# A pre-LayerNorm linear-attention and gated-GELU block on one core: centred first tiles with a ScalarE accumulator, a second ring for the weight tail, K weights first, joined late product groups

## The chip, the cores and the metric

The kernel runs on 1 core of one Trainium2 chip. The metric is device time in microseconds (us), as the median of several executions; "span" is the time from the first to the last instruction in a profiled execution, and is about 1.8 us shorter than the time of the same execution. A profile also gives the clock that the throttle granted TensorE; executions at clock 0.99 to 1.00 are called fast here and the one at clock 0.95 slow.

In the profile PE is TensorE's matmul stream, PEld its weight loads, DVE VectorE, ACT ScalarE, POOL GpSimd, and SPq the queue from which SyncE issues DMAs.

## The reference

Sequence 2048, width 448, 16 heads of 28, hidden width 1792, all in bfloat16.

```python
phi = lambda t: jnp.where(t > 0, t + 1, jnp.exp(t)) + 1e-6
q, k, v = split_heads(layernorm(x) @ wqkv)
pq, pk = phi(q), phi(k)
kv  = einsum("bhsd,bhse->bhde", pk, v)
den = einsum("bhqd,bhd->bhq", pq, pk.sum(s)) + 1e-6
h   = x + (einsum("bhqd,bhde->bhqe", pq, kv) / den) @ wo
y   = layernorm(h)
out = h + (gelu(y @ w_gate) * (y @ w_up)) @ w_down
```

## The kernel before

The sequence is cut into 16 tiles of 128 rows. The kernel makes a list of tasks, finds what depends on what from the buffers that they read and write, and places the tasks on each engine in a fixed order (five long lists of task numbers, one per engine). Each engine works through its list in order; a task that waits holds up all tasks behind it.

The head: statistics of each tile on VectorE, the reciprocal deviation on ScalarE (logarithm, then exponential), normalisation, and a transposition. Tiles 0 to 3 are transposed by TensorE, the others by a transposing DMA.

```python
def ln_tile(t):                                              # before
    ln_stats(t, ...)                                         # DVE: bn_stats, bn_aggr
    ln_rstd_act(t, ...)                                      # ACT: Ln, then Exp(-0.5 * .)
    if t < N_PE_TR:                                          # tiles 0..3
        op("dve", tensor_scalar(xnn, x_sb, mean, rstd, subtract, mult), "normD_t")
        # two transposes each on PE -> PSUM, evacuated by ACT ("evxA_t") and by DVE ("evxD_t")
    else:
        # GpSimd normalises ("normP_t"), a DMA transposes:
        G.add("sp", dma_start_transpose(xnT[:, t], xnn[:, i]), name="xT_t", after=[two])
# [cut]
def k_tile(t):
    # PE: K projection of tile t, 4 matmuls of 448 columns, "k_t"
    act_exp(activation(e1[:, i], psK, AF.Exp), "ek_t")
    op("dve", tensor_scalar(e1, e1, 1.0 + EPS, 0.0, min, max), "ck_t")
    op("dve", scalar_tensor_tensor(pk, psK, EPS, e1, max, add), "pk_t")
    # PE: x^T pk accumulated over the tiles, 4 matmuls, "pt4_t" (the last tiles: "pt3_t")
# [cut]  q_tile: projection "q_t", then ACT: Exp "eq_t" and Relu "rq_t"
```

After the last accumulation the sums are evacuated, the key-value product "kv" is made, masked to the heads, and multiplied with the output weights ("w2"). At the same time the denominators of the first tiles are started:

```python
op("act", ... "z1"); op("dve", ... "z0"); op("dve", ... "evpD_3")
# evpA_0, evpA_1 on ACT and evpD_2 on DVE bring the accumulated sums to SBUF; kv reads them all
# a2_pair: per pair of tiles
op("dve", tensor_scalar(eq, eq, 1.0, EPS, min, add), "cq_t")
op("dve", tensor_tensor(pq, pq, eq, add),            "aq_t")
op("dve" if t == 0 else "pool", tensor_tensor(t1, pq, zbc, mult), "t1_t")
op("dve", tensor_reduce(den, t1), "dr_t")
op("act", activation(den, den, AF.Identity, bias=eps), "deA_t")
```

The rest is a stream of attention outputs ("out"), gate/up pairs of 64-row matmuls ("gu", each pair on both halves of the array) and down projections ("down"). Between the last two, GpSimd normalises and VectorE copies a wrapped part of the row ("wrap_t").

## Time and profile before

| | value |
|---|---|
| time, median of 3 executions | 194.29 us (194.02 to 194.54) |
| profiled execution (slow) | 199.48 us, span 197.8 us, clock 0.95 |
| TensorE busy | 98% of the span |
| first projection starts (slow profile) | 6.31 us |
| key-value product starts (slow profile) | 38.76 us |

Of the page of the kernel before: the head line, TensorE's busy time, the granted clock by slices, the chain that ended last, and the costliest group of matmuls.

```profile
span 197.8 us, 4145 instructions
...
PE 193.7 (98%) x1572; PEld 106.9 (54%) x1572; DVE 132.0 (67%) x355; ACT 78.1 (39%) x226; POOL 50.7 (26%) x92
...
PEclk9999999999999999999999999999999999999999
...
PE 90%; DMA 4%; DVE 4%; POOL 1%; issue 0%; DVEq 0%; POOLq 0%
...
L605 PE MATMUL ps<-hnT,wgu_sb 64*128 64x512 bf16 (+1 forms) x490 | 89.9, 342 | 0.0
```

TensorE is the limit, and nearly all of the chain is TensorE. A change that leaves the products as they are can only take away waits. The clock row shows a 9 in every slice; the 0.95 comes from the run's list of cores. It can be seen in the matmuls too: one of 448 columns follows the next after 197 ns here and after 189 ns in the fast executions.

The timeline of the kernel before in the head (columns: start, duration, engine, line, operation, tiles, shapes; in brackets the idle time before and what ended it).

```profile
3.37 0.63 DVE L348 BATCH_NORM_STATS2 st<-x_sb 128x6 f32<-128x448 bf16 x1 [3.37 <-DMA x_sb<-in_A_x_dram]
...
4.24 0.29 ACT L355 ACTIVATE ln<-mv,eps_t 128x1 f32<-128x1 f32 x1 [1.75 <-DVE mv L349]
...
4.85 0.37 DVE L370 TENSOR_SCALAR xnn<-x_sb,mv,rs 128x448 bf16<-128x448 bf16 x1
...
5.37 0.38 PE L378 MATMUL ps<-ident,xnn 128*128 128x128 bf16 x4
...
6.31 0.74 PE L404 MATMUL ps<-wqk_sb,xnT 128*128 128x448 bf16 x3
```

From the landing of tile 0 at 3.37 us to the first projection at 6.31 us the work goes through VectorE, ScalarE, VectorE, TensorE, an evacuation and TensorE again. This is the stretch that the change attacks.

### The profile page before, as it was taken

What the parts mean: (1) busy time and instruction counts of PE and PEld (TensorE: products, weight loads), DVE (VectorE), ACT (ScalarE), POOL (GpSimd) and SP (SyncE); (2) the same over time, 40 slices, a digit from 0 to 9 for tenths busy, and PEclk for the clock granted to TensorE, in tenths of its full rate; (3) what the DMA queues carried; (4) which work ended last, traced back from release to release, by engine and by line L of the source; (5) the groups of instructions that cost most, each with busy time, mean ns of one, the idle gap of its engine ahead of it and who ended that gap; (6) DMA issues with size and microseconds to landing.
All of it is one profiled execution on the core that took longest, in us unless ns stands there. A gap on an engine that the chain in (4) does not pass through costs nothing.

```text
span 197.8 us, 4145 instructions
## 1 busy us (share of the span) xinstructions
PE 193.7 (98%) x1572; PEld 106.9 (54%) x1572; DVE 132.0 (67%) x355; ACT 78.1 (39%) x226; POOL 50.7 (26%) x92
## 2 busy tenths in 40 slices
PE   7999999999999999999999999999999999999995
PEld 7554555555767776654454445444444454444454
DVE  3899988999999989988786537244445422444412
ACT  3797645599943324141330420023444200334200
POOL 7067710640451955235222024000000000000000
PEclk9999999999999999999999999999999999999999
DMA  6966449994587046420217272600200010100011
GB/s 194 375 174 88 94 96 209 221 215 63 102 291 124 16 50 117 102 53 23 56 26 153 57 56 52 133 21 30 46 0 3 0 46 4 46 0 3 0 46 46
DMA packets 35331, 16.97 MB, mean 86 GB/s; under 512 B 27696, under 2 KB 34032, under 8 KB 35312
## 3 DMA queue, kind: packets, MB, share of 16 engines
q1 hardware_dynamic: 35168, 16.60, 38.4%
q8 instruction: 12, 0.20, 0.4%
q10 hardware_dynamic: 144, 0.11, 0.2%
q14 instruction: 7, 0.06, 0.1%
HBM read 8.26 MB, written 1.84 MB: 51 GB/s over the span
## 4 chain that ended last, share of the span: by engine, by line
PE 90%; DMA 4%; DVE 4%; POOL 1%; issue 0%; DVEq 0%; POOLq 0%
PE ps L603 42%; PE ps L575 22%; PE ps L404 9%; PE ps L523 7%; PE ps L423 5%; PE ps L605 3%; DMA x_sb<-in_A_x_dram 2%; DVE st L348 2%; DMA xnT<-xnn 2%; DVE pk L417 1%; PE ps L471 0%; PE ps L462 0%; POOL wqk_sb L302 0%; PE ps L550 0%; DVE xnn L370 0%; DVE mv L349 0%
## 5 line engine op out<-in xcount | busy, mean ns | idle before, releaser
L605 PE MATMUL ps<-hnT,wgu_sb 64*128 64x512 bf16 (+1 forms) x490 | 89.9, 342 | 0.0
L603 PE MATMUL ps<-hnT,wgu_sb 64*128 64x512 bf16 (+1 forms) x490 | 89.6, 342 | 0.0
L623 ACT ACTIVATE gl<-ps 128x256 bf16<-128x256 f32 x112 | 37.1, 381 | 88.5 <-PE ps L605 86.4
L603 PEld LDWEIGHTS ps<-hnT,wgu_sb 64*128 64x128 bf16 x490 | 46.3, 96 | 35.1 <-issue 3.1
L625 DVE TENSOR_TENSOR hh<-ps,gl 128x256 bf16<-128x256 f32 x112 | 42.5, 416 | 34.0 <-ACT gl L623 33.7
L605 PEld LDWEIGHTS ps<-hnT,wgu_sb 64*128 64x128 bf16 x490 | 45.2, 96 | 3.7 <-DVE hh L625 0.5
L575 PE MATMUL ps<-wd_sb,hh 128*128 128x448 bf16 (+1 forms) x238 | 45.2, 351 | 0.0
L575 PEld LDWEIGHTS ps<-wd_sb,hh 128*128 128x128 bf16 x238 | 23.3, 99 | 21.1 <-issue 1.3
L404 PE MATMUL ps<-wqk_sb,xnT 128*128 128x448 bf16 x128 | 28.2, 362 | 0.1
L488 POOL TENSOR_TENSOR t<-pq,zbc 128x448 f32<-128x448 bf16 x15 | 16.6, 1115 | 33.3 <-DVE pq L484 20.5
L579 DVE TENSOR_TENSOR x_sb<-ps,x_sb 128x448 bf16<-128x448 f32 (+1 forms) x17 | 10.0, 592 | 19.6 <-PE ps L575 19.6
L348 DVE BATCH_NORM_STATS2 st<-x_sb 128x6 f32<-128x448 bf16 x32 | 19.1, 612 | 3.5 <-DMA x_sb<-in_A_x_dram 3.4
L404 PEld LDWEIGHTS ps<-wqk_sb,xnT 128*128 128x128 bf16 x128 | 12.3, 99 | 12.1 <-DMA xnT<-xnn 0.5
L423 PE MATMUL ps<-pk,xnn 128*128 128x448 bf16 x64 | 14.4, 363 | 0.0
L523 PE MATMUL ps<-w,pqnT 112*128 112x448 bf16 x64 | 14.1, 362 | 0.0
L558 POOL TENSOR_SCALAR hn<-x_sb,nm,rs 128x448 bf16<-128x448 bf16 x14 | 10.9, 779 | 8.1 <-DMA hnT<-hn 7.4
L529 DVE TENSOR_TENSOR x_sb<-ps,x_sb 128x448 bf16<-128x448 f32 x16 | 9.5, 617 | 3.8 <-PE ps L523 3.8
L415 ACT ACTIVATE e<-ps 128x448 bf16<-128x448 f32 x16 | 8.7, 541 | 5.4 <-PE ps L404 3.6
L417 DVE SCALAR_TENSOR_TENSOR pk<-ps,e 128x448 bf16<-128x448 f32 x16 | 9.9, 616 | 0.2
L388 POOL TENSOR_SCALAR xnn<-x_sb,nm,rs 128x448 bf16<-128x448 bf16 x12 | 9.0, 749 | 3.5 <-ACT rs L357 3.5
L423 PEld LDWEIGHTS ps<-pk,xnn 128*128 128x128 bf16 x64 | 6.5, 101 | 6.2
L495 DVE TENSOR_TENSOR pqn<-pq,rd 128x448 bf16<-128x448 bf16 x16 | 9.6, 622 | 0.0
(65 smaller groups left out, 125.0 us busy)
## 6 DMA issues: line engine op xcount, KB each, us to landing
out_dram<-x_sb SPq DMA_DIRECT2D x15, 112.0 KB, 1.7
wd_sb<-in_B_w_down_dram SPq DMA_DIRECT2D x1, 1568.0 KB, 7.7
x_sb<-in_A_x_dram SPq DMA_DIRECT2D x3, 448.0 KB, 5.4
wgu_sb<-in_B_w_gate_dram SPq DMA_DIRECT2D x1, 896.0 KB, 11.9
wgu_sb<-in_B_w_up_dram SPq DMA_DIRECT2D x1, 896.0 KB, 16.5
wqk_sb<-in_A_wqkv_dram SPq DMA_DIRECT2D x1, 672.0 KB, 4.8
wgu_sb<-in_B_w_gate_dram SPq DMA_DIRECT2D x1, 672.0 KB, 6.0
wgu_sb<-in_B_w_up_dram SPq DMA_DIRECT2D x1, 672.0 KB, 8.4
```

Source lines behind the costliest of these rows:

```text
L348: op("dve", lambda e: e.bn_stats(st[:, t, :], src_ap), [b_src], [b_st[t]], "bnst%s_%d" % (tag, t))
L404: ins = e.matmul(ps[:, bk, 0:D], xnT[:, t, k, :], wqk_sb[:, k, c0:c0 + D], start=(k == 0), stop=(k == 3))
L417: op("dve", lambda e: e.scalar_tensor_tensor(pk[:, ip, :], psK, EPS, e1[:, i, :], ALU.max, ALU.add), [b_ps[bk], b_e1[i]], [b_pk[ip]], "pk_ ...
L423: ins = e.matmul(ps[:, BK_PT[c], 0:D], xnn[:, t % XN_R, c * 128:(c + 1) * 128], pk[:, ip, :], start=(t == 0), stop=(t == T - 1))
L488: op(eng, lambda e, t=t, n=n: e.tensor_tensor(t1[:, n, :], pq[:, t, :], zbc[:, :], ALU.mult), [b_pq[t]] + b_z, [b_t1[n]], "t1%s_%d" % (eng ...
L523: ins = e.matmul(ps[:, BK_OUT[n], 0:D], pqnT[0:GW, i2, n, g, :], w2[:, g, :], start=(g == 0), stop=(g == NG - 1))
L558: op("pool", lambda e, t=t, sh=sh: e.tensor_scalar(hn[:, sh, 0:D], x_sb[:, t, :], nm2[:, t:t + 1], rs2[:, t:t + 1], ALU.add, ALU.mult), [b ...
L575: ins = e.matmul(psO, hh[:, j, (t % HR) * 128:(t % HR + 1) * 128], wd_sb[:, j, c0:c1], start=(j == 0), stop=(j == NJ - 1))
L603: e.matmul(psG[:, jj * N:(jj + 1) * N], wgu_sb[A_, k, j * 128:(j + 1) * 128], hnT[A_, ka_, c0:c0 + N], start=(k == 0), stop=(k == NK - 1))
L605: ins = e.matmul(psU[:, jj * N:(jj + 1) * N], wgu_sb[B_, k, j * 128:(j + 1) * 128], hnT[B_, kb_, c0:c0 + N], start=(k == 0), stop=(k == NK ...
L623: G.add("act", lambda e, gi=gi, cs_=cs_, psG=psG: e.activation(gl[:, gi, cs_], psG[:, cs_], AF.Gelu_apprx_tanh), r=[b_ps[BK_G[i]]], w=[b_g ...
L625: op("dve", lambda e, dst=dst, srcU=srcU, srcL=srcL: e.tensor_tensor(dst, srcU, srcL, ALU.mult), [b_ps[BK_U[i]], b_glh], [b_ar[j_][t % HR] ...
```

## The change

Its intent: let TensorE start earlier and pause less.

1. Tiles 0 and 1 are only centred before the transposition; the reciprocal deviation becomes the per-partition scale of the later Exp and Relu. It drops out of the chain to the first projection. The K features of these two tiles then take a second ScalarE pass (rk_t) and an addition (pka_t). GpSimd normalises the two tiles besides (normP_0, normP_1), for the accumulation x^T pk.
2. Tile 1's statistics come from ScalarE's accumulator instead of VectorE.
3. The K half of the weights is loaded first, the weight tail goes by ScalarE's ring, and K0 and K1 are projected before Q0. The output weights are loaded after the transposing DMAs. The loads of x are cut smaller, and the padding of the weights moves from GpSimd to VectorE.
4. The orders of all engines are new. Late attention outputs stand next to down projections, so there are seven changes from full-height matmuls into the gate/up pairs and seven back, where there were nine and nine.

```diff
+    CEN = (0, 1)
+    ACT_ST = (1,)
-    WARM = 40
+    WARM, WARM2, NW2 = 30, 3, 3
-    SEQ = "Q0 K0 K1 Q1 K2 Q2 ..."
+    SEQ = "K0 K1 Q0 K2 Q1 Q2 ..."
@@ loads
-        dma_w3("sp", wqk_sb, 0, 2 * D, b_wqk, "dwqk")
-        dma_w1("sp", wqk_sb, 0, 2 * D, b_wqk, "dwqk_t")
-        dma_x("sp", 2, 4)
+        dma_wqk(1)
+        dma_w1("act", wqk_sb, 0, 2 * D, [None, b_wqt], "dwqk_t")
+        dma_x("sp", 2, 3)
+        dma_wqk(0)
+        dma_x("sp", 3, 4)
@@ ln_tile
+            if t in ACT_ST:
+                act_exp(... activation(e1[:, 2, :], x_sb[:, t, :], AF.Identity, scale=1.0 / D, accum_out=mv1[:, t, 0:1]) ... "asum")
+                act_exp(... activation(e1[:, 3, :], x_sb[:, t, :], AF.Square, scale=D ** -0.5, accum_out=mv1[:, t, 1:2]) ... "asq")
@@
+                if t in CEN:
+                    op("dve", ... tensor_scalar(xc[:, t % 2, 0:D], x_sb[:, t, :], mv1[:, t, 0:1], None, ALU.subtract) ... "cen")
@@ k_tile
+            sc = rs1[:, t:t + 1] if t in CEN else 1.0
+            if t in CEN:
+                act_exp(... activation(pk[:, ip, :], psK, AF.Relu, scale=sc) ... "rk")
+                op("dve", ... tensor_scalar(e1, e1, 1.0, EPS, ALU.min, ALU.add) ... "ck")
+                op("dve", ... tensor_tensor(pk, pk, e1, ALU.add) ... "pka")
[cut: q_tile the same way; ORDERS, five lists, are new throughout]
```

Three places of the new orders, given with the tasks' names in place of their numbers:

```diff
  VectorE, before:  cq_5 aq_4 aq_5 evpD_3 z0 t1_0 dr_0 rd_0 evpD_2 ...
  VectorE, after:   aq_4 evpD_3 cq_5 z0 aq_5 t1_0 dr_0 evpD_2 rd_0 ...
  TensorE, before:  k_8 pt4_5 pt4_6 k_9 k_10 pt4_7 ...
  TensorE, after:   k_8 pt4_4 k_7 pt4_5 k_9 k_10 pt4_6 ...
  ScalarE, after:   ek_0 rk_0 ek_1 ln1_3 rk_1 evxA_2 ...
```

## The prediction

> **What bounds the kernel now.** TensorE. The page has it busy 193.7 of 197.8 us; the chain of waits is 90% TensorE and stays on it from 18.3 to 195.4 us. In the list of its instructions matmuls start at stream pace (197 ns for 448 columns, 224 ns for a 512-column pair, at the granted clock 0.949). The profile is of a slow execution (199.48 us; timed runs 194.29), so I compare stages, not totals. The change leaves every product as it is: only the head and the bubbles can pay.
>
> **Where TensorE loses time** (start-to-start spacing less stream time):
> - Head: the first projection starts at 6.31 us. x tile 0 lands at 3.37; then statistics 0.63+0.18, logarithm and exponential 0.29+0.20, normalise 0.37, transposes, evacuation 0.38. Tile 1's normalise ends at 6.0. The QK weights land at 6.0, their tail at 6.3.
> - 0.28 us at 9.6 (normalised tile 3), 0.22 at 17.9 (transposing DMA of tile 7), 0.26 between 40 and 42.5.
> - Changes between full-height matmuls (attention output, down projection) and the 64-row gate/up pairs: nine into and nine out of the pairs, 92-105 ns each, 1.7 us together. The Trainium skill, "TensorEngine Tiling (Array Packing)", Key Properties, says that changing the tiling mode drains TensorE; these gaps agree.
>
> **What the change does.**
> 1. Tiles 0 and 1 are only centred; the reciprocal deviation becomes the scale of the later exp/relu. That takes 0.5 us of ScalarE and its hand-overs out of the head. Tile 1's sums go to ScalarE, idle then; VectorE saves 0.78 us. Half the weights (K) come first, so weights no longer bind. My sum: centring ends about 4.6 (tile 0) and 5.0 (tile 1); the warm-up matmuls (36 before the first transpose, 107 ns each from about 1.2) end about 5.05; transposes, evacuation 0.38: first projection at about 5.75, a gain of 0.55.
> 2. Given back in part: ScalarE gets two more 448-wide passes (0.43 us spacing each), VectorE still works without pause from 7 us; tile 3's normalised input comes about 10.4, a bubble near 0.35. At the first accumulation of K-features (11.78 before) I expect 11.3-11.5: gain 0.3-0.5.
> 3. The transposing DMAs start about when they did or slightly earlier, with the output projection's weights moved behind them; the 0.22 us bubble should go.
> 4. Joined groups: the two orders give seven changes into and seven out of the pairs. Four fewer at 95 ns: 0.38 us.
> 5. The end (last down projection, addition, store) is the same: 195.04 to 197.8.
>
> Sum: 0.4+0.2+0.4 = about 1.0 us, all on the critical path. **Predicted 193.3 us, range 192.2 to 194.5.** Chances: faster by over 2% 0.02, within 2% 0.96, slower by over 2% 0.02.
>
> **What would show it.** (1) First projection 5.6-5.9 us, K first. (2) First K-feature accumulation 11.3-11.5. (3) No gap over 100 ns for a transposing DMA near 18 us. (4) Seven gaps of about 95 ns into the pairs. (5) After the last pair eight down projections without a pause.
>
> **What would make it wrong.** TensorE's clock gate: the warm-up leaves half pace (107 to 56 ns per matmul) at 5.15 us. The Trainium skill, "TensorE: Matmul & The Clock Gate", Part 1, calls the window free-running (3.4 us), so an earlier start may run at half pace and save nothing. ScalarE's queue in the head may bind: projection banks come free later because two passes read each. A joined group may wait for an input that isn't ready, where before gate/up pairs filled the time. And a different granted clock in the timed runs moves the total as much as the change: 0.5% of clock is 0.9 us.

## More of the kernel before

In the run of the kernel before that was repeated later, the profile fell in a fast execution. Its timeline around the key-value product (L462) is the one to compare with:

```profile
35.15 0.39 DVE L450 COPY zbc<-zbc 64x448 f32<-64x448 f32 x1
35.57 0.62 DVE L488 TENSOR_TENSOR t<-pq,zbc 128x448 f32<-128x448 bf16 x1
35.62 2.48 POOL L488 TENSOR_TENSOR t<-pq,zbc 128x448 f32<-128x448 bf16 x2 [9.38 <-DVE zbc L450]
36.23 0.62 DVE L491 TENSOR_REDUCE den<-t 128x16 f32<-128x448 f32 x1
...
37.23 0.98 ACT L454 ACTIVATE pt_sb<-ps 128x448 bf16<-128x448 f32 x2
...
38.54 0.99 PE L462 MATMUL ps<-pt_sb,wv_sb 128*112 128x112 bf16 x16
```

VectorE's product for tile 0 (t1_0, the first L488) takes 0.62 us and starts just before GpSimd's for tile 1; the evacuations (L454) follow and the key-value product starts with no idle time in brackets.

## The result, and the profile after

The kernel after takes 195.12 us (median of 6, 194.93 to 195.19), the kernel before in the same rounds 194.27 us (194.02 to 194.76). The ratio is 1.0039 with a 95% interval of 1.0025 to 1.0053: within 2%, and slower by 0.4% where a gain of 0.5% was forecast; 195.12 lies outside the range. All ratios here are the mean time of one kernel's fast runs over that of the other's of the same rounds, so they are not quite the ratios of the quoted medians.

The profile after fell in a fast execution (195.09 us, clock 1.00). Of its page:

```profile
span 193.3 us, 4166 instructions
...
PE 187.3 (97%) x1571; PEld 112.7 (58%) x1571; DVE 132.5 (69%) x355; ACT 79.3 (41%) x232; POOL 51.9 (27%) x96
...
PE 89%; DVE 5%; ACT 2%; DMA 2%; issue 0%; SPq 0%; DVEq 0%; ACTq 0%
...
L648 PE MATMUL ps<-hnT,wgu_sb 64*128 64x512 bf16 (+1 forms) x490 | 86.5, 334 | 0.4 <-DVE hh L668 0.4
```

The span cannot be compared with the slow profile's 197.8 us. What can be read is the chain: ScalarE, absent before, is on it now with 2%. The last column of the last line has changed as well: gate/up matmuls idled 0.4 us for a product of VectorE, where the page before had 0.0.

The head of the kernel after:

```profile
3.32 0.63 DVE L365 BATCH_NORM_STATS2 st<-x_sb 128x6 f32<-128x448 bf16 x1 [1.71 <-DMA x_sb<-in_A_x_dram]
...
4.20 0.60 DVE L399 TENSOR_SCALAR xc<-x_sb,mv 128x448 bf16<-128x448 bf16 x2
...
5.05 0.39 PE L410 MATMUL ps<-ident,xc 128*128 128x128 bf16 x4
...
5.75 0.63 DVE L365 BATCH_NORM_STATS2 st<-x_sb 128x6 f32<-128x448 bf16 x1 [0.95 <-DMA x_sb<-in_A_x_dram]
...
5.89 0.54 PE L437 MATMUL ps<-wqk_sb,xnT 128*128 128x448 bf16 x2
...
6.30 0.27 DVE L417 COPY xnT<-ps 128x256 bf16<-128x256 bf16 x1
...
6.63 0.36 PE L437 MATMUL ps<-wqk_sb,xnT 128*128 128x448 bf16 x1 [0.20 <-DVE xnT L417]
```

The first projection starts at 5.89 us, as forecast. (Idle time in brackets counts from a modelled end of the matmul before; the waits that I quote are start-to-start spacing beyond the stream time of 189 ns for 448 columns, and come out larger by about 0.16 us.) After two of its four matmuls it stops: VectorE's half of the transposed tile (L417) stands behind the statistics of tile 2, whose rows had not landed before 5.7 us. From start to start the second matmul took 547 ns instead of 189: 0.36 us lost.

The next stop, at tile 2's projection, in the same timeline:

```profile
7.22 0.63 ACT L450 ACTIVATE e<-ps,rs 128x448 bf16<-128x448 f32 x1
...
7.75 0.63 ACT L452 ACTIVATE pk<-ps,rs 128x448 bf16<-128x448 f32 x1
...
8.27 0.64 ACT L450 ACTIVATE e<-ps,rs 128x448 bf16<-128x448 f32 x1
...
8.97 0.64 ACT L452 ACTIVATE pk<-ps,rs 128x448 bf16<-128x448 f32 x1
...
9.49 0.40 ACT L415 ACTIVATE xnT<-ps 128x256 bf16<-128x256 bf16 x1
...
9.94 0.93 PE L437 MATMUL ps<-wqk_sb,xnT 128*128 128x448 bf16 x4 [0.27 <-ACT xnT L415]
```

ScalarE goes through four scaled passes before it evacuates tile 2's transposes (L415); TensorE waits for that, 0.43 us from start to start beyond the stream time. And at the key-value product (L505):

```profile
35.15 0.39 DVE L493 COPY zbc<-zbc 64x448 f32<-64x448 f32 x1
35.57 0.39 DVE L527 TENSOR_TENSOR pq<-pq,eq 128x448 bf16<-128x448 bf16 x1
35.63 1.24 POOL L531 TENSOR_TENSOR t<-pq,zbc 128x448 f32<-128x448 bf16 x1 [9.82 <-DVE zbc L493]
35.88 1.46 DVE L531 TENSOR_TENSOR t<-pq,zbc 128x448 f32<-128x448 bf16 x1
...
37.38 0.62 DVE L534 TENSOR_REDUCE den<-t 128x16 f32<-128x448 f32 x1
...
38.03 0.31 ACT L536 ACTIVATE den<-den,eps_d 128x16 f32<-128x16 f32 x1 [2.60 <-DVE den L534]
...
38.25 0.96 ACT L497 ACTIVATE pt_sb<-ps 128x448 bf16<-128x448 f32 x2
...
39.30 1.00 PE L505 MATMUL ps<-pt_sb,wv_sb 128*112 128x112 bf16 x16 [0.67 <-DVE den L534]
```

Compare with the same place before. The addition aq_5 (L527) now stands between the copy z0 and t1_0. GpSimd's product for tile 1 is released by the copy as well and waits its turn beside aq_5, so it is next when aq_5 ends; VectorE's t1_0, recorded from 35.88 us, ends only 0.48 us after GpSimd's product and takes 1.46 us where it took 0.62. In the kernel before t1_0 came directly behind the copy, and it was GpSimd's product that took longer (1.48 us there; 1.04 us for most of the later ones). This holds in all 20 profiles: t1_0 took 1.46 us in the nine in which aq_5 stands between the copy and t1_0, and 0.62 to 0.63 us in the eleven in which it does not. Everything behind t1_0 moves: the reduction, ScalarE's addition of the epsilon (L536), which stands ahead of the two evacuations (L497), and the key-value product. TensorE waits 0.84 us. (The bracket of L505 names L534; of what the product reads, ScalarE's second evacuation, L497, ended last, at 39.21 us.)

The wait at tile 10, with the DMA queue's line for four transposing DMAs, tile 10's first:

```profile
19.74 5.33 SPq L423 DMA_TRANSPOSE xnT<-xnn  x4
...
23.34 0.92 PE L437 MATMUL ps<-wqk_sb,xnT 128*128 128x448 bf16 x4 [0.67 <-ACT e L450]
```

The bracket names a ScalarE pass, but the DMA of tile 10, issued at 19.74 us, landed at 23.21 us, 0.13 us before the projection started.

The sum of TensorE's waits up to the key-value product in this profile, each as start-to-start spacing beyond the stream time: 0.36 (first projection), 0.43 (tile 2), 0.18 (tile 5, for a ScalarE pass), 0.83 (tile 10, for its transposing DMA) and 0.84, together 2.64 us. In the fast profile of the kernel before they are 0.22, 0.08 and 0.93 (a transposing DMA again), 1.23 us. So 0.70 us of earlier start (5.89 instead of 6.59 in these two executions) are set against 1.41 us of new waits, and the key-value product starts 0.76 us later: 39.30 instead of 38.54. From there to the last matmul the kernel after takes 151.32 us and the kernel before 151.81.

### The profile page after: what moved, and what is told of

Its sections match the earlier page's. It is cut to its first block, busy times and chain, and to the rows that moved or that the text cites. A ratio compares the mean times of both kernels' runs of the same rounds, so it can differ in the third digit from the quotient of the medians.

```text
span 193.3 us, 4166 instructions
## 1 busy us (share of the span) xinstructions
PE 187.3 (97%) x1571; PEld 112.7 (58%) x1571; DVE 132.5 (69%) x355; ACT 79.3 (41%) x232; POOL 51.9 (27%) x96
## 4 chain that ended last, share of the span: by engine, by line
PE 89%; DVE 5%; ACT 2%; DMA 2%; issue 0%; SPq 0%; DVEq 0%; ACTq 0%
PE ps L646 30%; PE ps L618 22%; PE ps L648 13%; PE ps L437 10%; PE ps L566 7%; PE ps L463 5%; DMA x_sb<-in_A_x_dram 2%; ACT e L450 1%; DVE hh L668 1%; DVE t L531 1%; DVE hn L603 1%; DVE den L534 1%; ACT pk L452 1%; PE ps L505 1%; PE ps L514 0%; PE ps L593 0%
## 5 line engine op out<-in xcount | busy, mean ns | idle before, releaser
L648 PE MATMUL ps<-hnT,wgu_sb 64*128 64x512 bf16 (+1 forms) x490 | 86.5, 334 | 0.4 <-DVE hh L668 0.4
L646 PE MATMUL ps<-hnT,wgu_sb 64*128 64x512 bf16 (+1 forms) x490 | 86.4, 333 | 0.0
L646 PEld LDWEIGHTS ps<-hnT,wgu_sb 64*128 64x128 bf16 x490 | 45.3, 94 | 19.0 <-issue 2.6
L648 PEld LDWEIGHTS ps<-hnT,wgu_sb 64*128 64x128 bf16 x490 | 42.6, 94 | 9.9 <-DVE hh L668 5.7
L618 PE MATMUL ps<-wd_sb,hh 128*128 128x448 bf16 (+1 forms) x238 | 43.4, 342 | 0.0
L531 POOL TENSOR_TENSOR t<-pq,zbc 128x448 f32<-128x448 bf16 x15 | 16.0, 1079 | 34.8 <-DVE pq L527 19.8
L463 PE MATMUL ps<-pk,xnn 128*128 128x448 bf16 x64 | 13.7, 353 | 0.0
L566 PE MATMUL ps<-w,pqnT 112*128 112x448 bf16 x64 | 13.6, 353 | 0.0
L369 POOL TENSOR_SCALAR nm<-mv 128x1 f32<-128x1 f32 (+1 forms) x21 | 5.3, 257 | 29.1 <-DVE mv L366 28.7
L420 POOL TENSOR_SCALAR xnn<-x_sb,nm,rs 128x448 bf16<-128x448 bf16 x14 | 10.1, 724 | 5.6 <-ACT rs L374 4.2
L450 ACT ACTIVATE e<-ps 128x448 bf16<-128x448 f32 x14 | 7.6, 547 | 6.7 <-PE ps L437 5.2
```

What stands on the lines that cost most here:

```text
L420: op("pool", lambda e: e.tensor_scalar(xnn[:, i, 0:D], x_sb[:, t, :], nm1[:, t:t + 1], rs1[:, t:t + 1], ALU.add, ALU.mult), [b_x[t], b_nm1 ...
L463: ins = e.matmul(ps[:, BK_PT[c], 0:D], xnn[:, t % XN_R, c * 128:(c + 1) * 128], pk[:, ip, :], start=(t == 0), stop=(t == T - 1))
L531: op(eng, lambda e, t=t, n=n: e.tensor_tensor(t1[:, n, :], pq[:, t, :], zbc[:, :], ALU.mult), [b_pq[t]] + b_z, [b_t1[n]], "t1%s_%d" % (eng ...
L566: ins = e.matmul(ps[:, BK_OUT[n], 0:D], pqnT[0:GW, i2, n, g, :], w2[:, g, :], start=(g == 0), stop=(g == NG - 1))
L618: ins = e.matmul(psO, hh[:, j, (t % HR) * 128:(t % HR + 1) * 128], wd_sb[:, j, c0:c1], start=(j == 0), stop=(j == NJ - 1))
L646: e.matmul(psG[:, jj * N:(jj + 1) * N], wgu_sb[A_, k, j * 128:(j + 1) * 128], hnT[A_, ka_, c0:c0 + N], start=(k == 0), stop=(k == NK - 1))
```

## The experiments

There were eighteen runs, and every result was correct. "Order" diffs name tasks in place of their numbers. In each job the kernel before ran in the same rounds; its medians in the five jobs were 194.25, 194.06, 194.25, 194.22 and 194.59 us.

Theory H said that the loss is made in the head, up to the key-value product, and that the late reordering pays what was forecast for it. The rival, theory L, said that the joined late groups cost more than the saved mode changes. They are told apart by making each half alone.

### before_again and after_again

No edit; both kernels again, for a fast profile of the kernel before and for the spread.

> The kernel before, unchanged, to have its profile in the fast state (the first one was taken at a granted clock of 0.949, the kernel after at 1.0). Ratio 1.000 +- 0.002 on any theory. Theory A (my prediction read the bubbles off a slowed TensorE): at the full clock TensorE reaches every hand-over about 5% earlier and waits where the slow profile showed none; I expect a wait of 0.4 to 0.9 us before the key-value product (near 37 us) here too, a gap in the projections near 22 us, and more than 3 us lost in all, against 1.2 us outside the mode changes in the slow profile. Theory B (the change made new waits): none of those gaps is here, the key-value product starts without a wait as in the slow profile.

> The kernel after, unchanged, on the same chip as the three others, as a corner of a two-by-two comparison. All theories: ratio 1.003 to 1.005, as in the first measurement.

Measured: before_again 194.32 us, ratio 1.0004 (0.9984 to 1.0024). after_again 195.22 us, ratio 1.0056 (1.0040 to 1.0073), with the key-value wait and the 1.46 us of t1_0 as in the first profile. The loss repeats. Theory A of the first text falls in its main points: the kernel before has no wait at the key-value product at clock 1.00 either, and of its waits up to there, 1.23 us in sum, the one long one (0.93 us) is at tile 4, near 15 us, and none near 22 us. Theory B, that the change made new waits, stands.

### newhead_oldlate and oldhead_newlate

```diff
 newhead_oldlate: the kernel after
-  orders from the key-value product on: after's
+  orders from the key-value product on: before's
 oldhead_newlate: the kernel before
-  orders from the key-value product on: before's
+  orders from the key-value product on: after's
```

> The kernel after, but from the key-value product on each engine works in the order of the kernel before (nine mode changes again, attention outputs not joined). If the loss comes from the new order of the late part (theory L): 0.995 to 0.999 of before. If the loss comes from the head (theory H): 1.004 to 1.008. If both lose a little: about 1.002.

> The kernel before, but from the key-value product on each engine works in the order of the kernel after (seven mode changes, attention outputs joined to down projections). Theory L: 1.004 to 1.007 of before. Theory H: 0.996 to 0.999, as four mode changes of 95 ns (0.38 us, 0.2%) are saved.

Measured: newhead_oldlate 195.63 us, ratio 1.0072 (1.0050 to 1.0093); oldhead_newlate 194.09 us, ratio 0.9992 (0.9974 to 1.0009). With the four medians of this job the head costs 195.63 - 194.32 = 1.31 us with the old late part and 195.22 - 194.09 = 1.13 us with the new one, and the late part gives back 0.23 and 0.41 us. The two halves add up to within 0.2 us. Theory L falls, H stands: the loss is in the head. One thing this cut does not part: in newhead_oldlate aq_5 stands ahead of the copy z0, as in the kernel before, and t1_0 took 0.63 us; yet the key-value product waited 0.46 us and the product with the output weights 0.34 us (0.12 in the kernel before). VectorE was late there for another reason: cq_5 and aq_5 idled 0.78 and 0.23 us for ScalarE's eq_5 and rq_5, and z0 began at 35.66 us instead of 35.15. So the place of aq_5, taken up below, is the cause of the 0.84 us in the kernel after, and not the only way in which the new head makes the product wait.

Counted in the profiles, changes into the pairs cost 98 ns each and changes back 94 to 96 ns; there are nine and nine before, seven and seven with the new late order. The saving of 4 x 96 ns = 0.39 us is there. In oldhead_newlate most of it was spent again on one wait of 0.57 us, which is taken up under wrap_late.

### acc6_first, evac_first and both_moves

Two waits of the head, each removed by moving a task.

```diff
 acc6_first: TensorE's order
-  k_9 k_10 pt4_6 k_11
+  k_9 pt4_6 k_10 k_11
 evac_first: VectorE's order and ScalarE's order
-  t1_0 dr_0 evpD_2        deA_0 evpA_0 evpA_1
+  t1_0 evpD_2 dr_0        evpA_0 evpA_1 deA_0
 both_moves: both
```

> The kernel after, with one move in TensorE's order: the accumulation of tile 6 (its features ready at 21.2 us) stands before the K projection of tile 10 instead of after it. In the after kernel that projection waits from 22.5 to 23.3 us for its transposing DMA, which lands at 23.2. Theory order (the loss is made by where TensorE and the evacuations stand in the queues, not by the added operations): the wait is filled, 0.7 us gained, ratio to the kernel before about 1.001 instead of 1.005; the gap before tile 10's projection falls from 0.83 us to under 0.2. Rival theory work (the added ScalarE and VectorE operations are themselves the bound): the gain is lost again before the key-value product, ratio stays 1.004 to 1.006.

> The kernel after, with two moves before the key-value product: on VectorE the last evacuation of the accumulated banks goes ahead of the first denominator's reduction, on ScalarE the two evacuations go ahead of that denominator's epsilon. Theory order: the wait of 0.84 us before the key-value product falls to 0.1 or less, and after a part is given back at the first attention output, 0.5 to 0.8 us is gained: ratio about 1.001 to 1.002. Rival (the wait is set by the accumulation's end and the evacuations' own length): the wait stays over 0.5 us and the ratio over 1.004.

> Both moves together. Theory order: the gains add, 1.2 to 1.5 us, ratio 0.997 to 0.999: below the kernel before, near my prediction's 0.995. Rival work: 1.003 to 1.006. If the ratio is 0.999 to 1.000, equal to the run with the old head and the new late order (0.9992), then the new head (centring, ScalarE statistics, K first) is worth nothing even when its order is mended.

Measured: acc6_first 194.70 us, ratio 1.0042 (1.0021 to 1.0062). The wait of tile 10 was gone, but tile 8 waited 0.82 us for a transposing DMA that took 4.08 us. evac_first 195.37 us, ratio 1.0073 (1.0049 to 1.0096): the key-value wait went to zero and came back as 1.10 us before the product with the output weights, because the mask of the heads (kvm) stands behind other VectorE work. both_moves 194.84 us, ratio 1.0042 (1.0021 to 1.0064), with that 1.10 us wait and 1.18 us at tile 9 for a DMA of 4.83 us. None of the three came to the ratio that "theory order" gave it; another wait stood elsewhere each time.

Two lessons. Moving the evacuations does not mend the key-value wait while VectorE itself is late; the cause is ahead of it. And the tile that waits for a transposing DMA is not the same one in every execution.

### warm_more

A third theory: the earlier start is worthless, since TensorE arrives earlier only to wait for the transposing DMAs. Then a later start costs nothing.

```diff
-    WARM, WARM2, NW2 = 30, 3, 3
+    WARM, WARM2, NW2 = 40, 3, 3
```

> The kernel after with ten more warm-up matmuls, 0.5 to 0.6 us at 56 ns each, ahead of the first transposes, so that the first projection starts about 6.4 us, as late as in the kernel before. If the early start is hidden behind the transposing DMAs (tile 10's projection waits for its DMA anyway): no loss, ratio to before 1.004 to 1.006, as the kernel after. If the early start is worth its time: 1.007 to 1.008.

Measured: 196.36 us (4 runs), ratio 1.0117 (1.0097 to 1.0137). The first projection moved from 5.89 to 7.16 us, by 1.27 and not by the 0.5 to 0.6 expected, because the added matmuls still ran at half pace (107 ns apart until 6.8 us); the total moved by about 1.2 us. From the first projection to the key-value product this kernel took 33.40 us, the kernel after 33.41 us: the head shifts as a whole, though the single waits in it differ. The theory fell. The DMAs do not arrive at fixed times: their first one was issued at 12.18 instead of 11.28 us. The normalisations that feed them stand in the same engine orders as the work that was delayed.

### kv_fix

An attempt to mend VectorE's order around the key-value product in one go.

```diff
 VectorE's order
-  evpD_3 cq_5 z0 aq_5 t1_0 dr_0 evpD_2 rd_0 dr_1 pn_0 dr_2 kvm ...
+  evpD_3 z0 t1_0 cq_5 evpD_2 dr_0 aq_5 rd_0 dr_1 kvm pn_0 evwD_1 dr_2 ...
 ScalarE's order
-  deA_0 evpA_0 evpA_1
+  evpA_0 evpA_1 deA_0
[cut: later VectorE tasks moved too, dr_3 among them]
```

> The kernel after with the orders of VectorE and ScalarE rearranged just around the key-value product: the last accumulator evacuation and the two of ScalarE go first, the masking of the product follows directly on it, tile 5's query features and the second denominators later. The earlier try (two moves only) turned the 0.84 us wait before the product into one of 1.1 us before the output-weight products, because the masking stood behind five other VectorE operations. Theory order: both waits fall below 0.2 us, 0.6 to 0.9 us gained, ratio 1.000 to 1.002. Rival (TensorE's time there is bound by VectorE's sum of work, whatever its order): a wait of the same size shows up at the first attention output, ratio 1.004 to 1.006.

Measured: 199.43 us, ratio 1.0262 (1.0243 to 1.0282). The key-value wait was gone (38.93 us), but with dr_3 later, ScalarE's deA_3 waited for it and stood ahead of the evacuation of an attention output. TensorE waited 2.15 us for that, after another wait of 0.67 us shortly before, and then ran at half pace: nine matmuls of 448 columns came 370 to 374 ns apart instead of 189. The clock row of this page shows it, the 7 being the slice with the stretch:

```profile
PEclk9999999997999999999999999999999999999999
```

The granted clock is recorded as 0.50 from 46.79 to 50.21 us, 3.41 us, and as 1.00 before and after. In the 3.4 us before it TensorE was busy for 0.91 us. The half pace cost about 1.7 us more: here an idle spell on TensorE cost more than itself.

### no_scale and no_scale_look

To test whether the scaled passes are to blame: the arithmetic of before in the order of after.

```diff
-    CEN = (0, 1)
-    ACT_ST = (1,)
+    CEN = ()
+    ACT_ST = ()
```

> The kernel after with its head arithmetic undone: tiles 0 and 1 normalised before the transposes, tile 1's statistics on VectorE, no ScalarE sums, no relu passes for K features of tiles 0 and 1; K weights first, the tail ring, the split x loads and the after orders all stay. Theory work (ScalarE's added and lengthened passes, 0.53 us spacing with a per-partition scale against 0.43 us without, delay everything behind them): first projection about 0.5 us later, yet the first transposing DMA issues 0.2 to 0.6 us earlier, ratio 0.999 to 1.003. Theory order: the late start adds to the waits which stay, ratio 1.005 to 1.009.

> The run no_scale once more for its profile. It was 4 us slower than before, which neither theory gives. I expect a long TensorE gap in the first 10 us and then matmuls at half pace (373 ns for 448 columns instead of 189) for 3 to 7 us, that is the clock gate not yet released; rival: waits of over 2 us at one later step.

Measured: no_scale 198.16 us (median of five; one of them took 544.32 us, the others 198.06 to 198.30, and the profile fell in the one), ratio 1.0201 (1.0182 to 1.0220). The second look, 198.23 us, shows why it is slow: the projection of Q1 waited 1.18 us and that of Q2 1.93 us for a PSUM bank, which here is only freed by VectorE's pk_0 and pk_1, and these stand late in the order of after, where they were meant to be the additions that read no PSUM. My expectation of the clock gate was wrong; the rival in the same text (waits) was nearer, though it was two waits and neither over 2 us. The run says nothing of what the scaled passes cost in the head: arithmetic and order cannot be parted by undoing one of them. It does show that the key-value wait needs no scaled pass: with aq_5 in its new place t1_0 took 1.46 us and the product waited 0.83 us here too. In the 544 us execution TensorE's matmuls were slow from start to end (at the median 459 ns apart in the 448-column down projections, where 189 is usual, at a recorded clock of 1.00); why stays unexplained.

### xt_early

Start the transposing DMAs earlier: tile 5's deviation on GpSimd instead of ScalarE.

```diff
-                ln_rstd_act(t, ...)
+                (ln_rstd_pool if t == 5 else ln_rstd_act)(t, ...)
[cut: in the orders tile 4's negated mean goes behind tile 5's normalisation on GpSimd, and tile 6's aggregate and deviation come earlier]
```

> The kernel after with the chain of transposing DMAs started earlier: tile 5's reciprocal deviation by GpSimd's power instead of ScalarE's queue, tile 6's aggregate and deviation moved forward. If the transposing DMAs (one issue per 1.31 us) bound TensorE between 14 and 24 us: first issue 10.7 to 10.9 us instead of 11.0 to 11.3, the wait before tile 10's projection falls by 0.3 to 0.8 us, ratio 1.001 to 1.003. If they don't: ratio 1.004 to 1.006 and the wait stays.

Measured: 195.98 us, ratio 1.0098 (1.0079 to 1.0117). GpSimd's addition and power took 0.42 and 0.71 us, and the first transposing DMA was issued later (11.66 us), not earlier. The attempt failed, so it tests nothing.

### wrap_late

The 0.57 us wait in the new late order. Its place in oldhead_newlate, in the timeline of VectorE alone:

```profile
76.70 1.27 DVE L560 COPY hn<-hn 128x448 bf16<-128x448 bf16 x2
77.90 0.74 DVE L625 TENSOR_TENSOR hh<-ps,gl 128x256 bf16<-128x256 f32 x2
```

The two wrapping copies (L560) take 1.27 us together. The timeline of TensorE alone, of the same kernel:

```profile
78.02 0.27 PE L603 MATMUL ps<-hnT,wgu_sb 64*128 64x256 bf16 x1
78.70 0.28 PE L605 MATMUL ps<-hnT,wgu_sb 64*128 64x256 bf16 x1 [0.41 <-DVE hh L625]
```

The next pair idles for a product of gate and up (L625) that frees its bank. That product stands behind the wrapping copies, the second of which takes 1.11 us while GpSimd is in one of its own products (L488, 76.78 to 77.84 us). The edit moves the second copy, which nothing needs soon:

```diff
 oldhead_newlate, VectorE's order
-  wrap_5 wrap_4 hm0_10 ... rd_10 hm0_12
+  wrap_5 hm0_10 ... rd_10 wrap_4 hm0_12
```

> The old head with the new late order (ratio 0.9992 before), and one VectorE copy moved: tile 4's wrap copy took 1.11 us instead of 0.24 while GpSimd normalised, and a gate/up pair at 78 us waited 0.57 us for the product behind it. After the move (to an idle stretch of VectorE 2.7 us later) the wait should fall under 0.1 us and the ratio to 0.995 to 0.997. If the wait has another cause, or the transposed input of tile 4 comes too late, the ratio stays near 0.999.

("While GpSimd normalised" is a slip: the trace has the product, L488.)

Measured: 193.68 us (193.52 to 193.92), ratio 0.9971 (0.9956 to 0.9987). The same place:

```profile
77.13 0.24 DVE L560 COPY hn<-hn 128x448 bf16<-128x448 bf16 x1
77.62 0.89 DVE L625 TENSOR_TENSOR hh<-ps,gl 128x256 bf16<-128x256 f32 x2 [0.24 <-ACT gl L623]
```

One copy, 0.24 us, and the wait is gone. From the key-value product to the last matmul this kernel takes 151.09 us, where oldhead_newlate took 151.69 and the kernel before 151.81: 0.7 us is what the late order is worth without its own new wait. The same move takes 0.56 us off this stretch in the two other pairs of profiles that differ in it there (aq5_late 152.25 and aq5_wrap 151.69; aq5_last 151.61 and three_mends 151.05).

### aq5_late, aq5_wrap and aq5_wrap_acc6

The timeline of after suggests that aq_5 is the cause of the key-value wait. It is moved behind pn_0; then the wrap move and the pt4_6 move are added one at a time.

```diff
 aq5_late: the kernel after, VectorE's order
-  z0 aq_5 t1_0 dr_0 ... pn_0 dr_2
+  z0 t1_0 dr_0 ... pn_0 aq_5 dr_2
 aq5_wrap:      also  wrap_4 behind rd_10
 aq5_wrap_acc6: also  pt4_6 ahead of k_10
```

> The kernel after with one VectorE instruction moved: tile 5's addition of query features goes behind the first normalised query instead of standing between the denominator vector's copy and VectorE's first denominator product. Theory port (VectorE's product waited while GpSimd's, started first, held the operands' path): the product takes about 0.63 us instead of 1.46, the wait before the key-value product falls from 0.84 us to under 0.2, ratio 1.000 to 1.003. Rival (VectorE is simply full there): the product stays over 1.2 us or the wait moves to the next step, ratio 1.004 to 1.006.

> As aq5_late, and tile 4's wrap copy moved as in wrap_late. Both mends: another 0.5 us, ratio 0.997 to 1.000. If one of them only moves its wait: 1.001 to 1.004.

> As aq5_wrap, and tile 6's accumulation ahead of tile 10's projection. If the early head is worth its time once its order is mended: 0.994 to 0.997, at or below wrap_late's 0.9971. If the transposing DMAs take the gain back whatever the order: 0.998 to 1.001, above wrap_late.

Measured: aq5_late 195.51 us, ratio 1.0063 (1.0031 to 1.0094); aq5_wrap 194.99 us, 1.0032 (1.0002 to 1.0062); aq5_wrap_acc6 194.36 us, 1.0003 (0.9975 to 1.0032). In all three t1_0 took 0.62 to 0.63 us and the key-value product did not wait: the cause of that wait is confirmed. But in its new place aq_5 itself ran against GpSimd's next product and took 1.23 instead of 0.38 us, so the mask came late and the product with the output weights waited 1.16 us. The wait was moved again, not removed. The other two moves are worth about 0.5 and 0.6 us here, by the medians, but the intervals of neighbouring runs overlap.

### aq5_last and three_mends

aq_5 behind pn_3, where its delay holds up nothing; then with the two other moves.

```diff
 aq5_last: the kernel after, VectorE's order
-  z0 aq_5 t1_0 ... pn_3 hr_0
+  z0 t1_0 ... pn_3 aq_5 hr_0
 three_mends: also  wrap_4 behind rd_10,  pt4_6 ahead of k_10
```

> The kernel after with one VectorE addition (tile 5's query features) moved behind tile 3's normalised query, past the masking of the key-value product. Theory port: no wait over 0.2 us before the key-value product nor before the output-weight products, 0.8 to 1.0 us gained over after, ratio 1.000 to 1.002. Rival (VectorE is full there): the wait turns up at the first attention outputs, ratio 1.004 to 1.006.

> aq5_last, with tile 4's wrap copy late and tile 6's accumulation ahead of tile 10's projection. From aq5_wrap_acc6 (1.0003) another 0.5% should go: 0.995 to 0.997, as good as or better than the old head with the mended late order (0.9971), and what my prediction gave for the change (0.995). If the ratio stays over 0.999, the early head is worth nothing even mended.

Measured: aq5_last 195.32 us, ratio 1.0028 (1.0004 to 1.0051), over the forecast; it is not told apart from the kernel after (1.0039 and 1.0056), so this move alone is not shown to win time. The key-value wait was gone, and 0.12 us, as in the kernel before, were left before the product with the output weights; but in the profiled execution tile 10's projection waited 1.64 us beyond the stream time for its transposing DMA, which took 4.74 us from issue to landing:

```profile
22.14 0.92 PE L437 MATMUL ps<-wqk_sb,xnT 128*128 128x448 bf16 x4
24.54 0.92 PE L437 MATMUL ps<-wqk_sb,xnT 128*128 128x448 bf16 x4 [1.47 <-DMA xnT<-xnn]
```

three_mends 193.72 us (193.63 to 193.96), ratio 0.9947 (0.9926 to 0.9967). Around the key-value product:

```profile
35.10 0.39 DVE L493 COPY zbc<-zbc 64x448 f32<-64x448 f32 x1
35.52 0.63 DVE L531 TENSOR_TENSOR t<-pq,zbc 128x448 f32<-128x448 bf16 x1
35.57 2.47 POOL L531 TENSOR_TENSOR t<-pq,zbc 128x448 f32<-128x448 bf16 x2 [9.03 <-DVE zbc L493]
36.18 0.62 DVE L534 TENSOR_REDUCE den<-t 128x16 f32<-128x448 f32 x1
...
37.10 0.98 ACT L497 ACTIVATE pt_sb<-ps 128x448 bf16<-128x448 f32 x2
...
38.42 0.99 PE L505 MATMUL ps<-pt_sb,wv_sb 128*112 128x112 bf16 x16
```

These are nearly the lines of the kernel before again: 0.63 us for t1_0, no idle time before L505. The ratio is 0.56% under that of aq5_wrap_acc6 (1.0003, in another job), from which three_mends differs only in the place of aq_5; there the product with the output weights waited 1.16 us, here 0.12. With three task moves the changed kernel is faster than the kernel before by 0.5%, which is what I had forecast for the change as it stands; that the numbers meet is partly luck, as the late part gave 0.8 us here (151.05 us against 151.81) and not the 0.4 of the forecast. Its head took 32.14 us from the first projection to the key-value product, where the kernel after took 33.41 us. It started no earlier than the kernel before (6.28 us, as TensorE was still at half pace then), so in this execution the early start did not pay.

### The transposing DMAs over all profiles

Which tile waits differs from execution to execution. Over the 228 transposing DMAs in the head of the 19 profiles at hand (no_scale's, of the 544 us execution, left out), sorted by whether a packet of the kind "instruction" (16 KB in 0.9 to 1.5 us, or 8 KB in 0.3 to 1.8 us) was moving at any moment between issue and landing:

```
                          number   median   range (us from issue to landing)
no instruction packet        124     2.50    2.40 to 2.56
an instruction packet        104     3.03    2.40 to 5.13
```

Every DMA that took more than 2.56 us had one. That is a correlation, in all profiles, and no run varied the fetches by themselves. The fast profile of before had a packet near 13 and one near 21.7 us and waited 0.93 us at tile 4; the kernel after had three near 15, 21 and 22 us and waited at tile 10.

## Why the prediction was wrong, point by point

- **The limit.** TensorE bounds the kernel and only waits can be won: right. Every result here is a difference of waits, but for the half pace in kv_fix and the 544 us execution.
- **First projection at 5.6 to 5.9 us, K first: right.** It started at 5.89 and 5.84 us in the two profiles of after. In later kernels with the same warm-up and head it ranged from 5.57 to 6.28 us with the clock gate: 128-column matmuls were 56 ns apart from 4.2 us on in xt_early and still 107 ns apart at 6.07 us in aq5_last. The Trainium skill, "TensorE: Matmul & The Clock Gate", Part 1, calls the window free-running; these starts agree, and the risk was named in the prediction.
- **First K-feature accumulation at 11.3 to 11.5 us: not reliably.** 11.72 and 11.44 us. The old head gave 11.89, 11.51 and 11.65 in fast executions, not the 11.78 of the slow profile from which I had reckoned. Between the first projection and this step the new head lost what it had gained.
- **No gap for a transposing DMA: right for the place named, wrong in substance.** The gap near 18 us vanished and one of 0.83 us came at tile 10. Across the fast profiles one or two waits of 0.3 to 1.6 us for such a DMA fall on any of tiles 4 to 10, and the projection starts 0.05 to 0.14 us after the landing.
- **Seven changes of about 95 ns: right**, 94 to 98 ns. The Trainium skill, "TensorEngine Tiling (Array Packing)", Key Properties, says that a change of mode drains TensorE; the gaps agree, and are the same at clock 0.95 and 1.00.
- **The last down projections without a pause: right.**

**The step that failed** is "Sum: 0.4+0.2+0.4 = about 1.0 us, all on the critical path". The late 0.4 us was there (0.39 us, and with the wrap copy moved, a kernel that beats before by 0.3%). The head's 0.6 us was not: it became a loss of 1.1 to 1.3 us, measured with either late part. The start was earlier as forecast; what did not hold is that it stays won up to the key-value product. Two things went wrong in it, and a third in its baseline.

First, the term "given back in part" was too small. I put one bubble of 0.35 us. The profile shows 0.36 us in the first projection, because VectorE's evacuation stands behind the statistics of a tile that had not landed, 0.43 us at tile 2 behind four ScalarE passes, and 0.18 us at tile 5 behind another; the bubble at tile 3, where I had put it, did not appear. That ScalarE's queue might bind stood among the risks. I had reckoned 0.43 us spacing for a ScalarE pass of 448 columns; with a per-partition scale it is 0.53 us (0.63 long instead of 0.55). The Trainium skill, "ScalarE: Activation LUTs", What ACT_TABLE_LOAD costs, states about 93 ns for each per-partition pointer operand; the trace agrees (0.08 to 0.10 us), and I had not looked it up.

Second, I took the removal and read no waits that the new order makes of its own. The 0.84 us at the key-value product is one: an addition placed between z0 and t1_0 hands GpSimd the turn that t1_0 had. The Trainium skill, "SBUF — State Buffer", section "Who interferes with whom", says that a VectorE instruction with two SBUF inputs (against a GpSimd instruction that reads SBUF), or one in a 2-port performance mode, which a copy can enter, excludes GpSimd, that whichever comes first holds the port for its whole length, and that the order of issue decides who blocks. The trace agrees each time: t1_0 0.63 to 1.46 us, aq_5 0.38 to 1.23 us, the second wrapping copy 0.24 to 1.11 us, and GpSimd's product 1.04 to 1.48 us where it came second. This was there to be read in the diff of the orders. Shown by aq5_late and aq5_last, where nothing else was moved and t1_0 was 0.62 to 0.63 us again with no wait for the key-value product. What the runs show is the wait and how it goes; that the time is won as well is shown only with the other moves, by three_mends.

Third, I read the bubbles of before off a profile at clock 0.95. There TensorE is slower by 4% (197 ns for 448 columns instead of 189) and the other engines are not (t1_0 0.63 and 0.62 us), and the waits of the head were 0.28 and 0.22 us. At clock 1.00 the same kernel waited 1.23 us in one execution, and the same head 0.72 us in oldhead_newlate. This made my baseline wrong, but it does not explain the loss (theory A fell), and with one slow profile, and waits for DMAs that differ between fast ones too, how much the clock did to these waits is not shown.

What stays open: how much of the loss at tiles 4 to 10 belongs to the order and how much to when instruction packets happen to fall, as the two were never varied apart; whether three_mends (0.9947) and wrap_late (0.9971), of different jobs and with intervals that overlap, differ at all, that is, whether the new head is worth anything once mended; and what the scaled arithmetic costs by itself, since no_scale could not tell.

## What to carry to other kernels

In a kernel whose engines each work through a fixed order, cost a reordering by what each moved task now stands behind, not only by what it no longer delays: three single moves together made the difference between a loss of 0.4% and a gain of 0.5%. Where VectorE and GpSimd both read SBUF, ask at each hand-over who starts first, since a 0.4 us instruction in between made the next take 0.8 us longer here. Reckon waits from a profile at the clock of the timed runs, and when a mend moves a wait to the next step instead of removing it, look for the cause upstream.

## What the Trainium skill lacked or had wrong

- "Runtime: NRT & Kernel Launch", Instruction fetch mechanics, calls the cost of crossing a 16 KiB boundary mostly hidden. In these profiles instruction packets of 16 KB and 8 KB go with transposing DMAs that take up to 5.13 us instead of a median of 2.50, and every one that took more than 2.56 us had one in flight. It is a correlation; no run varied the fetches.
- "DMA: Bandwidth & Descriptors", DMA Transpose (X-bar), gives no latency for one small transposing DMA between SBUF tensors: 2.40 to 2.56 us here without such a packet, for 128 x 512 elements.
- "SBUF — State Buffer" says that who comes first holds the port. It does not say that a short VectorE instruction in between gives the turn away to a GpSimd instruction already waiting, so that the next VectorE instruction loses: 0.63 to 1.46 us for a 128 x 448 product with a 0.39 us addition ahead of it.
- "TensorE: Matmul & The Clock Gate", the part on oscillation, gives idle gaps of more than about 3.4 us as what brings half pace back. In kv_fix two waits, of 0.67 and 2.15 us within about 3 us (TensorE idle for 1.98 us in the longer), were enough: the granted clock is recorded as 0.50 for the 3.41 us that follow (373 ns for 448 columns), with TensorE busy for 0.91 of the 3.4 us before.
